# Hardware loops for VectorE and ScalarE in a decode attention kernel

## The chip, the cores and the metric

One core of one Trainium2 chip. The time is the device time of one execution in microseconds (us), measured in several executions; the kernel before takes 1277.7 us. The groups of experiments ran on different chips; each had the kernel before beside it on its own chip. A profile is one execution taken by the hardware profiler; its span is some 2 us shorter than the device time of the same run (1276.2 against 1278.06 us before). Where a text below says "fill", it is one transfer of 8 MB of the K or V cache into a slot of the ring.

## The reference

A gated mix of two branches for two single tokens. Branch A is attention over a cache: 16 query heads, 8 KV heads, 32768 cached positions, head size 256. Branch B is a small MLP with GELU.

```python
def _A_ref(x, k_cache, v_cache, wq, wo):          # x [2, 1, 448]
    q = (x @ wq).reshape(B, Sq, 16, 256).transpose(0, 2, 1, 3)
    k = jnp.repeat(k_cache, 2, axis=1)             # k_cache, v_cache [2, 8, 32768, 256] bf16
    v = jnp.repeat(v_cache, 2, axis=1)
    p = softmax(einsum("bhqd,bhkd->bhqk", q, k) * 256 ** -0.5)
    return einsum("bhqk,bhkd->bhqd", p, v).transpose(0, 2, 1, 3).reshape(B, Sq, 4096) @ wo
# ... b = MLP(x);  g = sigmoid((x * gate_w).sum(-1));  return g * a + (1 - g) * b
```

The K and V caches are 537 MB; everything else is 10.6 MB. So each byte of the cache is read once and used for very little arithmetic.

## The kernel before

The 16 pairs of batch and KV head are 16 "groups". A group has two K tiles and two V tiles of 8 MB. All of them pass through a ring of three slots in SBUF, loaded by SyncE in the order K2, V0, K3, V1 and so on. VectorE transposes the K tile in place (8 instructions), PE computes scores (`S`), VectorE and ScalarE do the softmax, PE multiplies with V (`PV`), VectorE picks out the result (`do_end`), and at the very end PE multiplies with wo (`FIN`).

Each engine's program is made by one Python function. Only PE's has a hardware loop in the kernel before: `loop` runs the body once in Python for the instructions, and waits use a register of the loop for the semaphore's value. The other engines' programs are unrolled.

```python
# _Eng.wait: inside a loop the value waited for is computed from the loop's register
if self.at is not None:
    nm, v0, d = next(self.at[1])
    self.eng.wait_ge(st.sem, self.at[0] * d + v0)
    return
# ... PE: 5 passes of 6 tiles, which is 3 groups
E.loop((NTILES - LAG) // UNIT, steps, ("dve", ("PT", 0)))
# ... VectorE, unrolled over all 64 tiles
for kind, idx in order:
    if kind == "K":
        for blk in range(NCK):
            T(idx, blk)                       # transpose in the ring
        if idx % NT == NT - 1:
            softmax(idx // NT)
    elif kind == "V" and idx % NT == NT - 1:
        do_end(idx // NT)
# ... ScalarE, unrolled over the 16 groups
for g in range(NG):
    chain(g)                                  # exp of the scores
    if g + 1 < NG:
        fill_A(g + 1)                         # 8 small copies of q for the next group's scores
# ... SyncE: a fill is issued when PE has released what lay in its slot
for d in order:
    for pd in before_of[d]:
        E.wait("pe", released(pd))            # K: last scores of the tile; V: last PV of the tile
```

## Time and profile before

| | before |
|---|---|
| time, median of 3 runs | 1277.68 us |
| span of the profiled run | 1276.2 us |
| read from HBM | 547.43 MB, 429 GB/s over the span |
| load queue (q1) | 99.4% of 16 engines' time |
| PE, VectorE, ScalarE busy | 57%, 54%, 3% |

The page of the profile gives the span, the busy time of each engine, then rows of 40 equal slices (tenths of busy time for the DMA engines, and GB/s), then for each DMA queue its packets, MB and share, then the engines of the chain that ended last.

```profile
span 1276.2 us, 8103 instructions
...
PE 725.7 (57%) x4683; PEld 165.2 (13%) x2155; DVE 690.8 (54%) x545; ACT 42.4 (3%) x182; POOL 2.5 (0%) x11
...
DMA  9999999999999999999999999999999999999997
GB/s 410 428 432 434 438 431 428 438 430 438 433 427 436 433 438 433 429 435 433 434 431 435 431 438 429 435 433 429 442 428 435 435 427 436 435 433 435 427 429 300
...
q1 hardware_dynamic: 12328, 547.43, 99.4%
q8 instruction: 9, 0.15, 0.0%
q14 instruction: 7, 0.06, 0.0%
...
DMA 58%; DVE 21%; PE 18%; ACT 2%; issue 1%; SPq 0%; another core or an unknown queue 0%
...
```

The load queue q1 is busy all the time and delivers 427 to 442 GB/s in each slice but the first and the last. Two queues called "instruction" also move bytes: the program itself, as the experiments will show (longer unrolled code raises q14's count from 7 to 14 or 15, PE's loop unrolled q8's from 9 to 27). They have 0.21 MB together, a share that rounds to 0.0%.

How far ahead are the loads? SyncE's timeline shows when fills were issued (start, duration of the issue, engine and line), VectorE's when a K tile's transposes began. Both are of the kernel before; in brackets stands how long the engine idled before an instruction and what ended that.

```profile
...
304.18 0.33 SPq L373 DMA_DIRECT2D ring<-in_A_k_cache_dram  x1
332.76 0.33 SPq L373 DMA_DIRECT2D ring<-in_A_v_cache_dram  x1
336.33 0.33 SPq L373 DMA_DIRECT2D ring<-in_A_k_cache_dram  x1
...
```

```profile
...
304.19 1.25 DVE L720 STREAM_TRANSPOSE PT<-pexp 128x1024 bf16<-128x1024 bf16 x1 [4.74 <-PE ps_o L322]
...
310.53 0.23 DVE L748 TENSOR_TENSOR attnT<-ps_m,rl 128x2 bf16<-128x2 f32 x2 [1.10 <-PE ps_m L492]
311.37 17.66 DVE L700 STREAM_TRANSPOSE ring<-ring 128x2048 uint32<-128x2048 uint32 x8 [0.60 <-DMA ring<-in_A_k_cache_dram]
350.06 11.08 DVE L700 STREAM_TRANSPOSE ring<-ring 128x2048 uint32<-128x2048 uint32 x5 [21.03 <-DMA ring<-in_A_k_cache_dram]
```

The K fill that is ahead of the V fill issued at 332.76 us lands at 350.06 us, when the transposes of its tile begin after 21 us of waiting for it. Only then is it the V fill's turn. So this fill was issued 17.3 us early, and a delay shorter than that should change nothing.

### The profile page before, as it was taken

The numbers are of one execution on the slowest core, as the hardware profiler recorded it, in microseconds if no ns is written. First come the engines' busy times: TensorE is split into PE (matmuls) and PEld (weight loads), VectorE is DVE, ScalarE is ACT, GpSimd is POOL, SyncE is SP. The second block draws the span as 40 slices with busy tenths as digits, with TensorE's granted clock in tenths as the row PEclk, the third lists the DMA queues.
The fourth block names the chain that finished last, engine by engine and source line by source line (L and its number), as shares of the span: only waits on it lengthen the run. The fifth ranks groups of instructions, "written<-read, shape, count | busy, mean of one in ns | idle before, by whom it ended". The sixth has DMA issues, their size and how long they took to land.

```text
span 1276.2 us, 8103 instructions
## 1 busy us (share of the span) xinstructions
PE 725.7 (57%) x4683; PEld 165.2 (13%) x2155; DVE 690.8 (54%) x545; ACT 42.4 (3%) x182; POOL 2.5 (0%) x11
## 2 busy tenths in 40 slices
PE   3566665645576454765536656455763547655464
PEld 3111111101011010111101111011110101111011
DVE  2775546745366553555735467453675535656351
ACT  1000000000000000000000000000000000000000
POOL 0000000000000000000000000000000000000000
PEclk9987887777887677887768877778886777876786
DMA  9999999999999999999999999999999999999997
GB/s 410 428 432 434 438 431 428 438 430 438 433 427 436 433 438 433 429 435 433 434 431 435 431 438 429 435 433 429 442 428 435 435 427 436 435 433 435 427 429 300
DMA packets 12520, 547.64 MB, mean 429 GB/s; under 512 B 1364, under 2 KB 3544, under 8 KB 3672
## 3 DMA queue, kind: packets, MB, share of 16 engines
q1 hardware_dynamic: 12328, 547.43, 99.4%
q8 instruction: 9, 0.15, 0.0%
q14 instruction: 7, 0.06, 0.0%
q10 hardware_dynamic: 176, 0.01, 0.0%
HBM read 547.43 MB, written 0.00 MB: 429 GB/s over the span
## 4 chain that ended last, share of the span: by engine, by line
DMA 58%; DVE 21%; PE 18%; ACT 2%; issue 1%; SPq 0%; another core or an unknown queue 0%
DMA ring<-in_A_k_cache_dram 56%; DVE ring L700 18%; PE ps_s L463 5%; PE ps_s L322 5%; PE ps_o L322 5%; DMA ring<-in_A_wo_dram 3%; PE ps_o L523 2%; DVE mx L704 1%; ACT pexp L616 1%; PE ps_m L485 1%; PE ps_m L480 1%; PE ps_m L475 0%; DVE gmax L706 0%; DVE ls L715 0%; DVE gmx L710 0%
## 5 line engine op out<-in xcount | busy, mean ns | idle before, releaser
L700 DVE STREAM_TRANSPOSE ring<-ring 128x2048 uint32<-128x2048 uint32 x256 | 565.1, 2275 | 319.2 <-DMA ring<-in_A_k_cache_dram 319.2
L463 PE MATMUL ps_s<-ring,Abd 128*128 128x512 bf16 x1024 | 428.9, 419 | 372.4 <-DVE ring L700 372.1
L322 PE MATMUL ps_s<-ring,Abd 128*128 128x512 bf16 x1024 | 425.3, 415 | 0.0
L463 PEld LDWEIGHTS ps_s<-ring,Abd 128*128 128x128 bf16 x1024 | 106.6, 104 | 786.2 <-DVE ring L700 410.9
L322 PE MATMUL ps_o<-ring,PT 128*24 128x512 bf16 x1504 | 128.4, 454 | 0.0
L523 PE MATMUL ps_o<-ring,PT 128*24 128x512 bf16 x544 | 64.8, 476 | 11.1 <-DMA ring<-in_A_v_cache_dram 11.1
L720 DVE STREAM_TRANSPOSE PT<-pexp 128x1024 bf16<-128x1024 bf16 x16 | 19.9, 1244 | 81.0 <-PE ps_o L322 81.0
L492 PE MATMUL ps_m<-sel,o_sb 128*128 128x2 f32 x64 | 16.2, 358 | 80.2 <-DVE o_sb L742 80.2
L742 DVE SCALAR_TENSOR_TENSOR o_sb<-ps_o,mask,o_sb 128x256 f32<-128x256 f32 x112 | 54.1, 483 | 9.6 <-PE ps_o L523 5.7
L704 DVE TENSOR_REDUCE mx<-ps_s 128x1 f32<-128x1024 f32 x16 | 19.6, 1224 | 60.1 <-PE ps_s L322 60.1
L612 ACT ACTIVATE negm<-ps_m 128x1 f32<-128x1 f32 x16 | 2.7, 171 | 1161.2 <-PE ps_m L480 1161.2
L523 PEld LDWEIGHTS ps_o<-ring,PT 128*24 128x24 bf16 x544 | 15.8, 107 | 119.7 <-issue 104.8
L492 PEld LDWEIGHTS ps_m<-sel,o_sb 128*128 128x128 f32 x64 | 14.9, 320 | 98.9 <-DVE o_sb L742 98.7
L485 PE MATMUL ps_m<-ls,ones_f 128*128 128x2 f32 x32 | 8.2, 325 | 28.2 <-DVE ls L715 28.2
L715 DVE TENSOR_SCALAR ls<-par,lsum 128x2 f32<-128x2 f32 x16 | 3.7, 228 | 31.1 <-ACT pexp L616 31.1
L475 PE MATMUL ps_m<-ident_f,mx 128*1 128x128 f32 x32 | 6.1, 270 | 23.6 <-DVE mx L704 23.6
L607 ACT COPY Abd<-qrep 32x16 bf16<-32x16 bf16 x128 | 19.4, 198 | 0.6
L616 ACT ACTIVATE pexp<-ps_s,negm 128x1024 bf16<-128x1024 f32 x16 | 17.8, 1114 | 0.5
L748 DVE TENSOR_TENSOR attnT<-ps_m,rl 128x2 bf16<-128x2 f32 x32 | 3.7, 158 | 21.2 <-PE ps_m L492 21.2
L739 DVE TENSOR_SCALAR o_sb<-ps_o,mask 128x256 f32<-128x256 f32 x16 | 7.1, 446 | 14.2 <-PE ps_o L322 14.2
L480 PE MATMUL ps_m<-ones_f,gmx 1*128 1x1 f32 x32 | 6.6, 271 | 9.9 <-DVE gmx L710 9.9
L485 PEld LDWEIGHTS ps_m<-ls,ones_f 128*128 128x128 f32 x32 | 6.8, 265 | 29.6 <-DVE ls L715 29.6
(65 smaller groups left out, 67.9 us busy)
## 6 DMA issues: line engine op xcount, KB each, us to landing
ring<-in_A_v_cache_dram SPq DMA_DIRECT2D x1, 4096.0 KB, 28.0
ring<-in_A_v_cache_dram SPq DMA_DIRECT2D x2, 2048.0 KB, 34.7
ring<-in_A_wq_dram SPq DMA_DIRECT2D x1, 3072.0 KB, 10.2
ring<-in_A_wo_dram SPq DMA_DIRECT2D x1, 1792.0 KB, 32.3
ring<-in_B_w_dram SPq DMA_DIRECT2D x1, 1568.0 KB, 18.0
ring<-in_B_w_dram SPq DMA_DIRECT2D x1, 1344.0 KB, 13.8
ring<-in_A_wo_dram SPq DMA_DIRECT2D x1, 1344.0 KB, 35.3
ring<-in_A_wq_dram SPq DMA_DIRECT2D x1, 512.0 KB, 11.0
```

The costliest lines, as they stand in the source:

```text
L322: return e.add_instruction(mybir.InstMatmult(name=f"I-{nc.next_id()}", engine=mybir.EngineType.PE, ldweights=False, ins=[e.lower_ap(x), e. ...
L463: fn = lambda e, o=o, x=x, st=st, sp=sp, s=s, w=w: e.matmul(o, a_win(s, w), x, start=st, stop=sp, skip_group_check=True)
L480: E.ins(lambda e: e.matmul(ps_m[:, C_BC:C_BC + 1], gmx[:, :], ones_f[0:1, 0:1], start=True, stop=True), key=("M2", g))
L485: E.ins(lambda e: e.matmul(ps_m[:, C_L:C_L + 2], ones_f[:, :], ls2[:, :], start=True, stop=True), key=("L", g))
L492: E.ins(lambda e, j=j: e.matmul(ps_m[:, C_OT + 2 * j:C_OT + 2 * j + 2], o_sb[:, j:Dh:2], sel[:, :], start=True, stop=True), key=(("OT", g) ...
L523: fn = lambda e, o=o, x=x, wt=wt, st=st, sp=sp, j=j: e.matmul(o, wt, x, start=st, stop=sp, skip_group_check=True)
L607: E.ins(lambda e, o=o, Q=Q, c=c: e.copy(o[:, :, c:c + 2], qrep[32 * Q:32 * Q + 32, :, kvh, :, b]), key=(("A", g) if (Q == 3 and c == 16) e ...
L616: E.ins(lambda e: e.activation(pexp[:, :].rearrange("p (r i a) -> p i r a", r=CR, i=2), ps_s[:, :].rearrange("p (i r a) -> p i r a", i=2, ...
L700: E.ins(lambda e: e.transpose(k_words(idx, blk), k_words(idx, blk)), key=("T", idx, blk))
L704: E.ins(lambda e: e.tensor_reduce(mx[:, :], ps_s[:, :], AX.X, ALU.max), key=("MX", g))
L720: E.ins(lambda e: e.transpose(PT[:, :], pexp[:, :]), key=("PT", g))
L742: E.ins(lambda e, p=p, m=m: e.scalar_tensor_tensor(out=o_sb[:, :], in0=p, scalar=m, in1=o_sb[:, :], op0=ALU.mult, op1=ALU.add), key=(("OS" ...
```

## The change

VectorE gets a hardware loop of 5 passes of three groups, as PE has; ScalarE one of 14 passes of one group. The columns of `qrep` (read by ScalarE) and `attnT` (written by VectorE) that belong to a group must then be an address computed from the loop's register. For that both tiles are laid out so that a step of one group is a constant step in columns. The two products that write `attnT` become one of four columns, for which sums and reciprocals are four wide and the latter's tile is threefold. The intent is a shorter program.

```diff
+    def dyn(self, base, step):
+        return base if self.at is None else self.at[0] * step + base
...
-        qrep = sb("qrep", [P, NS, Hkv, 2, Bn], dt.bfloat16)
+        qrep = sb("qrep", [P, NS, 2 * NG], dt.bfloat16)
-        attnT = sb("attnT", [P, Hkv, 2, 2, Bn], dt.bfloat16)
+        attnT = sb("attnT", [P, 4 * NG], dt.bfloat16)
...
 # PE, final product: the two weight columns are now 64 bytes apart
-   ps_a[32 * q:32 * q + Bn, :], attnT[:, kvh, j, hh, :],
+   ps_a[32 * q:32 * q + Bn, :], attnT[:, 4 * kvh + 2 * j + hh:4 * NG:4 * Hkv],
...
 # ScalarE
-   E.ins(lambda e, ...: e.copy(o[:, :, c:c + 2], qrep[32 * Q:32 * Q + 32, :, kvh, :, b]), ...)
+   E.ins(lambda e, ...: e.copy(o[:, :, c:c + 2],
+                               qrep[32 * Q:32 * Q + 32, :, bass.ds(E.dyn(2 * g, 2), 2)]), ...)
-            for g in range(NG):
-                chain(g)
-                if g + 1 < NG:
-                    fill_A(g + 1)
+            def step(n):
+                chain(n + 1)
+                fill_A(n + 2)
+            chain(0)
+            fill_A(1)
+            E.loop(NG - 2, step, ("dve", ("PT", 0)))
+            chain(NG - 1)
...
 # VectorE
-                for j in range(2):
-                    E.ins(lambda e, j=j: e.tensor_tensor(
-                        attnT[:, kvh, j, :, b], ps_m[:, C_OT + 2 * j:C_OT + 2 * j + 2], rl[g % 2][:, :], ALU.mult), ...)
+                E.ins(lambda e: e.tensor_tensor(attnT[:, bass.ds(E.dyn(4 * g, 4 * UNIT // NT), 4)],
+                                                ps_m[:, C_OT:C_OT + 4], rl[g % 3][:, :], ALU.mult), key=("O", g))
-            for kind, idx in order: ...
+            for i in range(LAG):
+                K(i)
+            E.loop((NTILES - LAG) // UNIT, steps, ("dve", ("PT", 0)))
+            do_end(NG - 1)
```

(Cut: the four-wide `par`, `ls2`, `rl` and `L`, and waits on constants inside a loop.)

More of the change, by code (lines that the diff above doesn't have):

```diff
@@ L59, in loop @@
             v0 = v[1] - d
-            assert v0 > 0 and d > 0 and all(v[i] == v0 + i * d for i in range(1, n)), reqs
+            assert v0 > 0 and d >= 0 and all(v[i] == v0 + i * d for i in range(1, n)), reqs
             assert v[0] in (None, v0) or (nm == first[0] and v0 < v[0] <= ev[first[1]]), reqs
@@ L93, in wait @@
             assert nm == stream
-            self.eng.wait_ge(st.sem, self.at[0] * d + v0)
+            self.eng.wait_ge(st.sem, self.at[0] * d + v0 if d else v0)
             return
@@ L226, in bass_gated_mix__gqa_block_cached__dense_activation_gelu__decode_kernel @@
         sel = sb("sel", [P, 2], dt.float32)
-        par = sb("par", [P, 2], dt.float32)
+        par = sb("par", [P, 4], dt.float32)
         mx = sb("mx", [P, 1], dt.float32)
@@ L232, in bass_gated_mix__gqa_block_cached__dense_activation_gelu__decode_kernel @@
         lsum = sb("lsum", [P, 1], dt.float32)
-        ls2 = sb("ls2", [P, 2], dt.float32)
-        rl = [sb(f"rl{i}", [P, 2], dt.float32) for i in range(2)]
+        ls2 = sb("ls2", [P, 4], dt.float32)
+        rl = [sb(f"rl{i}", [P, 4], dt.float32) for i in range(3)]
         ps_s = pm("ps_s", [P, 1024], dt.float32)
@@ L484, in L @@
                 E.wait("dve", ("LS", g))
-                E.ins(lambda e: e.matmul(ps_m[:, C_L:C_L + 2], ones_f[:, :], ls2[:, :],
+                E.ins(lambda e: e.matmul(ps_m[:, C_L:C_L + 4], ones_f[:, :], ls2[:, :],
                                          start=True, stop=True), key=("L", g))
@@ L593, in prog_act @@
             E.wait("pe", "QR")
-            E.ins(lambda e: e.copy(qrep[:, :, :, :, :].rearrange("p s v h b -> p s (v h b)"), ps_qr), key="qr")
+            E.ins(lambda e: e.copy(qrep[:, :, :].rearrange("p s (b n) -> p s n b", b=Bn),
+                                   ps_qr.rearrange("p s (n b) -> p s n b", b=Bn)), key="qr")
             E.wait("act", "qr")
@@ L606, in fill_A @@
                     for c in (0, 16):
-                        E.ins(lambda e, o=o, Q=Q, c=c: e.copy(o[:, :, c:c + 2], qrep[32 * Q:32 * Q + 32, :, kvh, :, b]),
+                        E.ins(lambda e, o=o, Q=Q, c=c: e.copy(o[:, :, c:c + 2],
+                                                            qrep[32 * Q:32 * Q + 32, :, bass.ds(E.dyn(2 * g, 2), 2)]),
                               key=(("A", g) if (Q == 3 and c == 16) else None))
@@ L639, in prog_dve @@
             E.ins(lambda e: e.tensor_reduce(sel[:, :], ident_f[:, :].rearrange("p (c h) -> p h c", h=2), AX.X, ALU.add), key="sel")
-            E.ins(lambda e: e.tensor_reduce(par[:, :], ident_f[:, :].rearrange("p (k h) -> p h k", h=2),
-                                            AX.X, ALU.add), key="par0")
-            E.wait("dve", "par0")
-            E.ins(lambda e: e.tensor_scalar(par[:, :], par[:, :], 0.5, None, op0=ALU.mult), key="par")
+            E.wait("dve", "sel")
+            for j in range(2):
+                E.ins(lambda e, j=j: e.tensor_scalar(par[:, 2 * j:2 * j + 2], sel[:, :], 0.5, None, op0=ALU.mult),
+                      key=("par" if j else "par0"))
             E.wait("pool", "xm0")
@@ L716, in softmax @@
                 E.wait("pe", ("L", g))
-                E.ins(lambda e: e.reciprocal(rl[g % 2][:, :], ps_m[:, C_L:C_L + 2]), key=("RL", g))
+                E.ins(lambda e: e.reciprocal(rl[g % 3][:, :], ps_m[:, C_L:C_L + 4]), key=("RL", g))
                 if g >= 1:
@@ L725, in do_end @@
                     E.wait("pe", ("PV", g * NT + NT - 1))
-                if g >= 1:
-                    E.wait("pe", ("OT", g - 1))
+                E.wait("pe", ("OT", g - 1))
                 for n in range(8):
@@ L746, in do_end @@
                 E.wait("dve", ("RL", g))
-                for j in range(2):
-                    E.ins(lambda e, j=j: e.tensor_tensor(
-                        attnT[:, kvh, j, :, b], ps_m[:, C_OT + 2 * j:C_OT + 2 * j + 2], rl[g % 2][:, :], ALU.mult),
-                        key=(("O", g) if j == 1 else ("O0", g)))
+                E.ins(lambda e: e.tensor_tensor(attnT[:, bass.ds(E.dyn(4 * g, 4 * UNIT // NT), 4)],
+                                                ps_m[:, C_OT:C_OT + 4], rl[g % 3][:, :], ALU.mult), key=("O", g))
             gelu1()
@@ L754, in prog_dve, with K, steps @@
             do_bp()
-            for kind, idx in order:
-                if kind == "K":
-                    for blk in range(NCK):
-                        T(idx, blk)
-                    if idx % NT == NT - 1:
-                        softmax(idx // NT)
-                elif kind == "V" and idx % NT == NT - 1:
-                    do_end(idx // NT)
+            def K(idx):
+                for blk in range(NCK):
+                    T(idx, blk)
+                if idx % NT == NT - 1:
+                    softmax(idx // NT)
+            def steps(n):
+                for i in range(UNIT * n, UNIT * n + UNIT):
+                    K(i + LAG)
+                    if i % NT == NT - 1:
+                        do_end(i // NT)
+            for i in range(LAG):
+                K(i)
+            E.loop((NTILES - LAG) // UNIT, steps, ("dve", ("PT", 0)))
+            do_end(NG - 1)
             E.wait("pe", "FIN")
```

## The prediction

> **What bounds it.** The transfers. The page's header and its DMA queue part show 547.4 MB read in 1276.2 us, the load queue busy for 99.4% of 16 engines' time; in the 40-slice view DMA is 9 in all slices but the last. Four fills of the ring (33.55 MB) take 77.4 us (transposes of K tiles start at 195.26 and 272.66 in the timeline): 433.5 GB/s. [...] VectorE is busy 54%, ScalarE 3%. The chain of waits gives DMA 58%.
>
> **The margin of the queue.** A V fill is issued at 332.76 us; the K fill ahead of it lands at 350.06: 17.3 us early. Others I followed: V fills 17 to 18 us, K fills some 26, the last V tile 18 (issued 1225.45, its turn at 1243.7), wo 27. VectorE idles about 34 us of each 77.4 us group. So a delay within a group is paid back by idle time unless it passes some 17 us, and does not add up.
>
> **What the change does.**
> - VectorE: 5 passes of 3 groups, ScalarE: 14 of one; waits and two addresses come from registers. The trace times no register work. PE already loops 5 times; at its turn (310.5 to 315.9 us) there is only a wait for VectorE, so a turn costs under 5.4 us there. My estimate for VectorE: under 5 us for a turn and under 4 us of register work along a group's chain (about 20 waits), together below 17.
> - Two 158 ns products per group become one: 0.1 us of VectorE per group. Sums and reciprocal are 4 wide instead of 2 (228 and 170 ns: same). Setup of `par` hides under the wq load.
> - ScalarE: 8 copies per group (1.25 us together) with a register column. Even at 0.3 us more each, Abd, ready at 144.9 us, is first read at 161: 16 us of margin.
> - Instruction fetch: 0.21 MB on instruction queues, 0.5 us at 433 GB/s. Shorter program or refetch: within 0.3 us either way.
> - Tail: the last load lands at 1271.44, then 1.73 us of matmuls, 0.33 mix, 2.6 store. The last product ends at 1271.02, off the path by 0.4 us; one instruction instead of two: 0.07 us earlier. The final matmuls read two weight columns 64 bytes apart instead of adjacent; 64 loads of 22 ns follow the last landing: 0 to 0.5 us.
>
> **On the critical path:** practically nothing; -0.3 to +0.7 us.
>
> **Prediction:** 1277.7 us, 8 in 10 between 1275 and 1281. Faster by over 2%: 0.01; within 2%: 0.97; slower by over 2%: 0.02.
>
> **What would show it.** Load queue still about 99.4%, 433 GB/s in every middle slice. Issue to landing of the fills (46.7 us K, 36.6 V median) shorter by the loop's delay, a few us, but well above 19.3 us, the time of one fill. VectorE busy about 2 us less; new small gaps before its transposes after each third group and before each small softmax operation. The last load lands within 1 us of 1271.4.
>
> **What would make it wrong.** A turn or register waits costing over 17 us (fetching the body behind the loads, say): then slices with DMA under 9 appear at the 5 turns, and the time grows by 5 times the excess. Strided weights costing much in the tail.

-0.3 to +0.7 us is 0 to 0.5 for the strided weights, 0.07 less for the product and 0.3 either way for the instruction fetch. The bounds for a turn, the register work and the strided weights were estimates.

## The result, and the profile after

| | before | after |
|---|---|---|
| time, median (range) of 4 runs | 1277.70 us (1277.58 to 1277.82) | 1275.64 us (1275.06 to 1276.38) |
| ratio, 95% interval | | 0.9984, 0.9967 to 1.0002 |
| span of the profiled run | 1276.2 us | 1274.3 us |
| VectorE busy | 690.8 us | 690.2 us |
| packets and MB on q14 | 7, 0.06 | 2, 0.02 |

A ratio is the mean time of one kernel's runs over that of the other's of the same rounds, so it is not quite the ratio of the medians. The interval just touches 1; a second group of five runs, below, gave 0.9984 again with 0.9970 to 0.9997. So there is a gain of 2 us, small and real, at the lower edge of what was predicted. The changed kernel's runs fall in two clusters, near 1275.1 and 1276.3.

The page of the kernel after, the same lines:

```profile
span 1274.3 us, 8475 instructions
...
PE 724.8 (57%) x4683; PEld 165.7 (13%) x2155; DVE 690.2 (54%) x529; ACT 43.3 (3%) x182; POOL 2.5 (0%) x11
...
DMA  9999999999999999999999999999999999999998
GB/s 411 428 432 433 438 433 430 434 435 431 434 432 430 440 434 430 436 430 430 442 432 432 434 430 430 442 432 432 434 432 430 440 432 432 434 432 430 440 423 323
...
q1 hardware_dynamic: 12328, 547.43, 99.5%
q8 instruction: 9, 0.15, 0.0%
...
q14 instruction: 2, 0.02, 0.0%
...
DMA 58%; DVE 18%; PE 18%; issue 4%; ACT 1%; ACTq 0%; SPq 0%; another core or an unknown queue 0%
...
```

The gain is not in VectorE's work. It comes in steps. The table of windows below (kernel before) is cut at the issue of the V fill that ends a group, so that each row is one group; it shows the window, its length, the busy time and count of instructions of PE, weight loads, VectorE, ScalarE and GpSimd, the granted clock, the DMA share and GB/s.

```profile
...
371.45:449.51 78.06, 43.96 (x266) 9.25 (x106) 42.67 (x32) 2.49 (x11) 0.00 (x0) 0.76 1.00 433
449.51:526.79 77.28, 44.12 (x266) 9.44 (x106) 42.57 (x32) 2.49 (x11) 0.00 (x0) 0.78 1.00 433
604.21:682.59 78.38, 43.56 (x266) 9.18 (x106) 42.66 (x32) 2.49 (x11) 0.00 (x0) 0.78 1.00 432
914.83:993.21 78.38, 43.56 (x266) 9.17 (x106) 42.67 (x32) 2.49 (x11) 0.00 (x0) 0.78 1.00 434
...
```

The same four groups of the kernel after:

```profile
...
371.46:448.86 77.40, 45.03 (x266) 9.46 (x106) 42.51 (x31) 2.49 (x11) 0.00 (x0) 0.76 1.00 434
448.86:526.27 77.41, 43.70 (x266) 9.33 (x106) 42.61 (x31) 2.49 (x11) 0.00 (x0) 0.78 1.00 433
603.67:681.08 77.41, 44.89 (x266) 9.47 (x106) 42.52 (x31) 2.48 (x11) 0.00 (x0) 0.76 1.00 433
913.27:990.67 77.40, 43.50 (x266) 9.30 (x106) 42.61 (x31) 2.48 (x11) 0.00 (x0) 0.78 1.00 434
...
```

After, every group takes 77.4 us. Before, three of these four groups are 0.7 to 1.0 us longer, while DMA share, PE and VectorE are as in the others. Something takes 1 us of the loads without showing up in their share.

The trace holds the landing times of each fill: its semaphore is raised 16 times, as many times as the page counts load engines. I sorted these 16 times for each fill, which the views of the profile don't do, and set them beside the start times of the instruction packets, which are in the trace too. "Lag" is the time from the first to the last of the 16.

```
fill   before: landed  step   lag   |  after: landed  step   lag
 19           369.39  19.35  1.86   |        369.40  19.36  2.10
 20           389.25  19.86  2.36   |        388.75  19.35  2.09
 32           621.50  19.36  2.39   |        620.95  19.35  2.04
 33           641.82  20.32  3.37   |        640.30  19.35  2.04
 48           932.12  19.36  3.41   |        930.56  19.36  1.98
 49           952.44  20.32  4.39   |        949.90  19.34  1.97
 63          1223.38  19.35  4.39   |       1220.82  19.35  1.91
 64          1243.69  20.31  5.35   |       1240.17  19.36  1.91
8 KB packets of q14 while the loads run, start in us:
before   86.89  301.90  385.39  625.87  934.07  1078.93  1239.83
after    91.24  302.65
```

All other fills from 20 to 64 take 19.33 to 19.37 us in both. The four steps of the kernel before (0.51, 0.97, 0.97 and 0.96 us) come in fills during which an 8 KB piece of the program was fetched (at 385.39, 625.87, 934.07 and 1239.83 us), and the lag grows by nearly the same amount each time: one load engine falls behind, the other fifteen do not. (The trace does not name the engine of a landing. But the second last of the 16 stays 1.8 to 1.9 us after the first in all eight fills of the kernel before, so it is one engine, and the same one, that is last.) (The pieces at 301.90 and 1078.93 us make no step. They are ScalarE's, as the experiments will show, and fell on an engine that was not the last: in the sorted times of the kernel before one landing falls back from 0.18 to 0.82 us after the first between fills 15 and 16, and from 0.78 to 1.38 us between fills 55 and 56.) In fill 64, the last whole one before the pieces of the tail, fifteen engines are within 1.9 us of each other, and one is 3.5 us behind these. By these numbers a packet of q14 holds up the loads of one engine, here by 0.5 to 1.0 us; how an engine shares its time between two queues was not shown. (PE's program comes on q8, as pe_flat below will show.)

A fill is 128 packets of 65536 bytes in the trace of the kernel before, and 15 of its 16 landings at fill 64 come within 1.9 us of each other; this fits an even split, 8 packets for each engine. So the last load ends when the slowest engine does. The end of the program then follows: in the kernel before the span ends 3.7 us after the last landing, in the kernel after and in after_again 3.8 us. The tail, seen on PE, before and then after:

```profile
...
1268.14 1.66 PE L537 MATMUL ps_f<-ring,attnT 128*2 128x112 bf16 x64 [3.01 <-DMA ring<-in_A_wo_dram]
1269.73 1.01 PE L492 MATMUL ps_m<-sel,o_sb 128*128 128x2 f32 x4
1271.44 1.73 PE L537 MATMUL ps_f<-ring,attnT 128*2 128x112 bf16 x64 [0.69 <-DMA ring<-in_A_wo_dram]
```

```profile
...
1264.64 1.66 PE L541 MATMUL ps_f<-ring,attnT 128*2 128x112 bf16 x64 [3.02 <-DMA ring<-in_A_wo_dram]
1266.23 1.01 PE L496 MATMUL ps_m<-sel,o_sb 128*128 128x2 f32 x4
1268.10 1.29 PE L541 MATMUL ps_f<-ring,attnT 128*2 128x112 bf16 x48 [0.85 <-DMA ring<-in_A_wo_dram]
1270.61 0.55 PE L541 MATMUL ps_f<-ring,attnT 128*2 128x112 bf16 x16 [1.22 <-DMA ring<-in_A_wo_dram]
```

64 final matmuls take 1.66 us in both (first line of each), so the weight columns that are now 64 bytes apart cost nothing. The last piece of wo landed at 1272.49 before and at 1270.48 after, by the landing times; fifteen of the engines were done at 1269.18 and 1269.17.

The loop itself shows in VectorE's timeline of the kernel after at the first turn, the jump back to the start of the body (the same place as shown of before):

```profile
...
305.02 1.25 DVE L730 STREAM_TRANSPOSE PT<-pexp 128x1024 bf16<-128x1024 bf16 x1 [5.32 <-PE ps_o L326]
...
311.57 0.16 DVE L756 TENSOR_TENSOR attnT<-ps_m,rl 128x4 f32 x1 [1.30 <-PE ps_m L496]
312.10 17.67 DVE L710 STREAM_TRANSPOSE ring<-ring 128x2048 uint32<-128x2048 uint32 x8 [0.36 <-issue]
350.07 11.08 DVE L710 STREAM_TRANSPOSE ring<-ring 128x2048 uint32<-128x2048 uint32 x5 [20.30 <-DMA ring<-in_A_k_cache_dram]
```

The turn leaves a gap of 0.36 us with the reason "issue"; the trace's compare-and-branch there takes 63 ns (56 to 67 at the four turns). The wait before the product, now with a computed address, went from 1.10 to 1.30 us. Along the whole chain of the group, which starts at the same time in both (294.06 and 294.04 us), the product starts 1.0 us later than before (311.57 against 310.53).

### The profile page after: what moved, and what is told of

The parts are those of the page before. It is cut to its first block, busy times and chain, and to the rows that moved or that the text cites. A ratio compares the mean times of both kernels' runs of the same rounds, so it can differ in the third digit from the quotient of the medians.

```text
span 1274.3 us, 8475 instructions
## 1 busy us (share of the span) xinstructions
PE 724.8 (57%) x4683; PEld 165.7 (13%) x2155; DVE 690.2 (54%) x529; ACT 43.3 (3%) x182; POOL 2.5 (0%) x11
## 3 DMA queue, kind: packets, MB, share of 16 engines
q1 hardware_dynamic: 12328, 547.43, 99.5%
HBM read 547.43 MB, written 0.00 MB: 430 GB/s over the span
## 4 chain that ended last, share of the span: by engine, by line
DMA 58%; DVE 18%; PE 18%; issue 4%; ACT 1%; ACTq 0%; SPq 0%; another core or an unknown queue 0%
DMA ring<-in_A_k_cache_dram 55%; DVE ring L710 16%; PE ps_s L467 5%; PE ps_s L326 5%; PE ps_o L326 5%; DMA ring<-in_A_wo_dram 3%; PE ps_o L527 2%; DVE mx L714 1%; PE ps_m L489 1%; PE ps_m L484 1%; PE ps_m L479 0%; ACT pexp L622 0%; DVE gmax L716 0%; DVE ls L725 0%; DVE gmx L720 0%
## 5 line engine op out<-in xcount | busy, mean ns | idle before, releaser
L496 PEld LDWEIGHTS ps_m<-sel,o_sb 128*128 128x128 f32 x64 | 14.9, 321 | 98.5 <-DVE o_sb L751 98.3
L489 PE MATMUL ps_m<-ls,ones_f 128*128 128x4 f32 x32 | 9.1, 354 | 29.4 <-DVE ls L725 29.4
L725 DVE TENSOR_SCALAR ls<-par,lsum 128x4 f32<-128x4 f32 x16 | 3.7, 229 | 32.6 <-ACT pexp L622 32.6
L612 ACT COPY Abd<-qrep 32x16 bf16 (+1 forms) x128 | 19.4, 198 | 0.6
L756 DVE TENSOR_TENSOR attnT<-ps_m,rl 128x4 f32 (+1 forms) x16 | 2.6, 162 | 24.2 <-PE ps_m L496 24.2
```

The source lines that it names most:

```text
L489: E.ins(lambda e: e.matmul(ps_m[:, C_L:C_L + 4], ones_f[:, :], ls2[:, :], start=True, stop=True), key=("L", g))
L496: E.ins(lambda e, j=j: e.matmul(ps_m[:, C_OT + 2 * j:C_OT + 2 * j + 2], o_sb[:, j:Dh:2], sel[:, :], start=True, stop=True), key=(("OT", g) ...
L612: E.ins(lambda e, o=o, Q=Q, c=c: e.copy(o[:, :, c:c + 2], qrep[32 * Q:32 * Q + 32, :, bass.ds(E.dyn(2 * g, 2), 2)]), key=(("A", g) if (Q = ...
```

## The experiments

Two theories stood against each other after the result, and two smaller ones. **Fetch**: what the loop saves is 8 KB pieces of VectorE's program, each of which costs about 1 us of one load engine, the same each time. **Layout**: the new layout saves time. **ScalarE**: its loop does. **Lottery**: chance of this load of the program. All kernels below gave correct results.

### Which part of the change gives the gain

Four kernels on one chip, 5 rounds each. `loop` is told to emit the passes one after the other for some engines; everything else stays as in the changed kernel.

```diff
     def loop(self, n, body, first):
         self.wait(*first)
+        if self.name in ('act', 'dve'):      # no_loop; ('act',) in dve_loop, ('dve',) in act_loop
+            for i in range(n):
+                body(i)
+            return
```

(Waits for events of a group before the first are skipped when unrolled.)

> The changed kernel again, as the control of this group. Fetch theory (each 8 KB piece of VectorE's program that is fetched while the loads run takes about 0.96 us of one load engine, always the same one, and the last load ends with its slowest engine): 1275.0 to 1276.4 us, ratio 0.998 to 0.999 to the kernel before; in the trace no instruction packet on queue 14 between 310 us and the end of the loads, and a spread of the 16 landings of a fill of about 2 us late in the run (5.3 us in the kernel before). Lottery rival (the 2 us is chance of this one load of the program): anywhere between 1275 and 1278.

> Changed layout, VectorE looped, ScalarE unrolled. Fetch theory: as the changed kernel, 1275.0 to 1276.5 us, since ScalarE's fetches (two, near 302 and 1079 us in the kernel before) hit another load engine that had 0.8 us and more to spare; VectorE's own fetches after 310 us are gone. Layout rival (the 2 us comes from the new layout of q and attention, not from loops): 1275.6. ScalarE rival (its loop is what helps): 1277.7.

> Changed layout, ScalarE looped, VectorE unrolled. Fetch theory: about as the kernel before, 1277.0 to 1278.0 us, with four or five fetches of 8 KB for VectorE and a spread of the landings of 4 to 5.4 us at the end of the loads. Layout rival and ScalarE rival: 1275.6.

> Changed layout, neither VectorE nor ScalarE looped. Fetch theory: as the kernel before, 1277.0 to 1278.0 us, spread of the landings 4 to 5.4 us at the end. Layout rival: 1275.6. If all four kernels of this group scatter over 1275 to 1278 without order, the lottery rival stands.

| | median (range), us | q14 packets from 310 us to the end of the loads | lag at fill 64 | span |
|---|---|---|---|---|
| before (9 runs beside) | 1277.54 (1277.33 to 1278.08) | 5 | 5.35 | 1276.2 |
| after_again | 1275.36 (1275.26 to 1276.28) | 0 | 2.38 | 1273.5 |
| dve_loop | 1274.98 (1274.89 to 1276.44) | 1 | 2.19 | 1273.2 |
| act_loop | 1277.82 (1277.68 to 1277.91) | 4 | 4.11 | 1276.0 |
| no_loop | 1277.62 (1277.47 to 1277.68) | 5 | 3.64 | 1275.7 |

(Packets, lag and span are of the profiled run; for before, of the profile above.) In act_loop and no_loop a last q14 packet at 1259 us brings the lag to 5.1 and 4.7 after fill 64. The layout alone gives nothing, ScalarE's loop gives nothing, VectorE's loop gives all of it: layout, ScalarE and lottery theories fall. dve_loop and after_again can't be told apart: each has runs in both clusters. The four also tell whose packets are whose: with ScalarE unrolled there are packets near 302 and 1077 us, with VectorE unrolled near 387, 688, 936 and 1259.

### Dose: more program, hardly more work

If the fetches are the cause, a longer program must cost time in proportion, although what it does costs the engine nothing that matters. Instructions that write one element were added; four kernels on one chip, 3 rounds.

```diff
 # bef_dve_pad (unrolled) and aft_dve_pad (in the loop): after the product of each group but the last
+                    for k in range(64):
+                        E.ins(lambda e, k=k: e.memset(junk[0:1, k:k + 1], 0.0))
 # bef_act_pad: at the end of fill_A
+                for k in range(64):
+                    E.ins(lambda e, k=k: e.copy(junk[0:1, k:k + 1], ident_f[0:1, 0:1]))
 # pe_flat: the changed kernel with PE's loop unrolled too
+        if self.name in ('pe',): ...
```

> The kernel before (VectorE unrolled) with 64 more one-element writes on VectorE after each group's last product, 15 times: 960 instructions, 60 KB more of program, which is 7.5 more fetches of 8 KB. Fetch theory: 7.5 times 0.96 us on the load engine that already ends last: 1277.6 + 7.2 = 1284.8 us (1283 to 1286), spread of the landings at the end of the loads about 12.5 us instead of 5.3. Rival that the time follows VectorE's own work and waits, or that instruction fetches are too few bytes to matter: unchanged, 1277.6 (the writes take about 4 us per group, inside the 17 us margin).

> The changed kernel (VectorE looped) with the same 64 writes per group, inside the loop. Fetch theory: if the body of some 300 instructions and their register work is kept on chip from pass to pass, 1275.3 to 1276.5; if it is fetched anew in each pass (about 3 pieces of 8 KB, 4 more passes), about 12 more fetches, up to 1287. Either way the time follows the count of queue 14's packets in the trace at 0.96 us each. Rival (VectorE's work): as for the other kernel with pads, the same change of time there and here.

> The kernel before with 64 more one-element copies on ScalarE after each fill of the block-diagonal tile, 16 times: 64 KB more of program, 8 more fetches of 8 KB. Fetch theory: ScalarE's fetches go to another load engine, that ended 4 us before the last one; 8 fetches at 0.6 to 1.0 us push it past by 1 to 4 us: 1278.5 to 1281.5 us, less than the same pads on VectorE cost. If all program fetches go to one engine: 1285. Rival: unchanged, 1277.6.

> The changed kernel with PE's loop unrolled: about 286 KB more of program, some 18 more fetches of 16 KB. In the trace so far each 16 KB fetch of PE delayed one load engine by about 1.5 us, each time another. Fetch theory with the engines taken in turn: 18 times 1.5 spread over 16 engines, about 1.7 us more for all: 1276.5 to 1279 us. If they all went to one engine: over 1295. If fetches don't matter: 1275.4.

| | median (range), us | ratio to before | q14 packets in the loads (before: 7) | q8 packets (before: 9) |
|---|---|---|---|---|
| bef_dve_pad | 1284.09 (1284.06 to 1284.56) | 1.0052 | 14 | 9 |
| aft_dve_pad | 1295.05 (1294.87 to 1295.22) | 1.0136 | 23 | 9 |
| bef_act_pad | 1279.46 (1279.39 to 1279.78) | 1.0015 | 15 | 9 |
| pe_flat | 1279.09 (1278.90 to 1279.61) | 1.0011 | 2 | 27 |

**bef_dve_pad.** 7 more packets, 6.4 us more. The 64 writes take 1.8 us of VectorE per group (timeline below). In the landing times, nine fills are 0.95 to 0.99 us longer than 19.35, each at one of the packets, and the lag at fill 64 is 11.74 us: one engine 9.5 us behind the other fifteen. The line of q14 on its page (packets, MB, share):

```profile
...
q14 instruction: 14, 0.11, 0.0%
...
```

**aft_dve_pad.** The same writes in the loop made it slower by 11 us than the same writes unrolled. The reason is in the same line: 23 packets against 14.

```profile
...
q14 instruction: 23, 0.19, 0.0%
...
```

The time follows the count: 20 packets between 310 us and the end of the loads against none in the changed kernel, 19.7 us more than its 1275.36, so 0.98 us each. (The changed kernel was not in this group; 1275.36 is from the chip where the kernel before took 1277.54 us, here it took 1277.70.) My guess of 12 packets was too low: the trace has five for each pass. VectorE's timeline of this kernel around a turn:

```profile
...
548.62 0.16 DVE L757 TENSOR_TENSOR attnT<-ps_m,rl 128x4 f32 x1 [1.30 <-PE ps_m L497]
548.72 1.79 DVE L761 MEMSET junk<- 1x1 f32 x64
558.27 2.31 DVE L711 STREAM_TRANSPOSE ring<-ring 128x2048 uint32<-128x2048 uint32 x1 [7.76 <-issue]
563.93 15.47 DVE L711 STREAM_TRANSPOSE ring<-ring 128x2048 uint32<-128x2048 uint32 x7 [3.35 <-issue]
```

At the turn VectorE itself now waits 7.8 us with the reason "issue", and 3.4 us more after the first transpose. So a body of 346 instructions (rows of one pass of VectorE in the trace) is fetched anew in each pass, some of it more than once by estimate (the 60 to 64 bytes per instruction worked out below make less than three packets, and five come). The wait alone is inside the margin of 17 us; the time is lost on the load engine. The lag at fill 64 is 7.6 us and not 20, because the other engines, up to 10.7 us ahead, ran out of issued loads soon after a turn (the first landings of fills 31, 43 and 55 come 4.5 to 4.8 us late, and the load queue's share fell to 98.3%). The last engine's fills are 0.9 to 1.0 or 2.9 us late, one packet or three.

**bef_act_pad.** 8 more packets, 1.8 us more. The line of q14:

```profile
...
q14 instruction: 15, 0.12, 0.0%
...
```

The steps of the landing times are 0.67 to 0.70 us here. Sorted, the landings of fill 64 show two laggards, one 6.9 us after the first engine (ScalarE's) and one at 4.0 (VectorE's); in the kernel before VectorE's was last and ScalarE's among the others. So the two programs are fetched by different load engines, and the cost shows only once its engine is the last.

**pe_flat.** 18 more pieces of 16 KB on q8, 3.7 us more than the changed kernel (again the 1275.36 us of the other chip). Its two instruction queues:

```profile
...
q8 instruction: 27, 0.44, 0.1%
...
q14 instruction: 2, 0.02, 0.0%
...
```

Eight engines end with a lag of 4.4 us or more in fill 64, eight with 2.1 us or less. The fills are late (by 1.5 to 1.7 us) only at fills 20, 41 and 63: after the 9th, 17th and 25th packet of q8. (The 1.5 us of the expectation: in the kernel before, with a packet of q8 at 62.61 us, one landing falls back from 0.39 to 1.94 us after the first between fills 3 and 4.) This fits PE's program being fetched by eight engines in turn, one about 1.6 us later each time (the trace does not name them); an estimate of 18 times 1.6 over 8 is 3.6 us, near the 3.7 measured. I had expected sixteen engines in turn and 1276.5 to 1279 us, and the median is just outside. 288 KB of program, spread over eight engines by this reading, cost PE less than 56 KB on one engine cost VectorE.

### How large may a loop's body be

The changed kernel's VectorE body has 154 rows in the trace and is not fetched again; 346 rows are. One more kernel has 26 writes per group in place of 64 (232 rows). And ScalarE's 64 copies went into its own loop (21 rows become 85).

```diff
 # aft_dve_pad26                                  # aft_act_pad: the changed kernel, at the end of fill_A
+                    for k in range(26):          +                for k in range(64):
+                        E.ins(... memset ...)    +                    E.ins(... copy ...)
```

> The changed kernel with 26 instead of 64 one-element writes on VectorE per group, inside the loop: a pass is 232 rows of VectorE in the trace, between the changed kernel's 154 (not fetched again) and 346 with 64 writes (about five fetches of 8 KB per pass, 1295 us). Fetch theory: the time follows the count of queue 14's packets, 1275.0 to 1276.5 us if a body of 232 stays on chip, and about 0.96 us more for each packet between 310 us and the end of the loads if not (12 to 20 packets: 1286 to 1295). It can't say which; this brackets the size of a free body. Rival that the writes themselves cost what the 64 cost: 26/64 of 19.7 us, 1283.4 us.

> The changed kernel with the 64 one-element copies on ScalarE inside its loop of one group per pass. The body is then some 80 instructions. Fetch theory, if such a body stays on chip from pass to pass as the changed kernel's VectorE body of some 145 instructions does: no fetches for ScalarE after 310 us, 1275.0 to 1276.5 us, against 1279.5 for the same copies unrolled. If it is fetched anew: as unrolled or slower, 1279 or more.

aft_dve_pad26: 1276.07 us (1275.04 to 1276.75), ratio 0.9990 (0.9973 to 1.0006); aft_act_pad: 1275.61 us (1274.70 to 1276.33), ratio 0.9982. Both stay with the changed kernel, and neither has a q14 packet between 310 us and the end of the loads. The line of q14 of aft_dve_pad26:

```profile
...
q14 instruction: 2, 0.02, 0.0%
...
```

78 writes more per pass cost nothing when the body is not fetched again (the rival's 1283.4 us is far off), and the same 64 copies of ScalarE that cost 1.8 us unrolled cost nothing in the loop. A body of 232 rows is free, one of 346 is not. In these runs VectorE's program comes in packets of 8192 bytes. Unrolled, it fetches one per four groups (625.87 to 934.07 us), and the windows count 32 instructions per group, so 64 bytes each (the 960 writes of bef_dve_pad took 7 packets more, 60 bytes each); by this estimate a body of 232 is 15 KB and is not fetched again, and one of 346 is 22 KB and is. Where between the two the limit lies, and what sets it, was not measured. (A row of the trace need not be exactly one instruction of the program.) PE, whose body of three groups is some 1100 rows (three times 266 and 106 in the windows), fetches at most one packet between its first turn and the tail in the kernels where it is looped.

### Is the margin of 17 us real

The prediction rests on it, so it was measured: VectorE gets two or five long reductions after each group's product, in the loop, which delays the next K tile's transposes. They add few instructions.

```diff
+                if g < NG - 1:
+                    for k in range(2):              # delay10; 5 in delay25
+                        E.ins(lambda e, k=k: e.tensor_reduce(
+                            junk[:, k:k + 1], PT[:, :].rearrange("p (n o) -> p n o", o=1).to_broadcast([P, 1024, 4]),
+                            AX.XY, ALU.max))
```

> The changed kernel with two more long reductions on VectorE after each group's product (4096 elements each; the row maximum takes 1.22 us for 1024, so an estimate of 4.9 us each): the next K tile's transposes start some 9.8 us later, 15 times. The prediction's margin theory: a V fill is issued some 17 us before its turn, so nothing changes: 1275.0 to 1276.5 us. Rival that VectorE's delays reach the end of the chain: up to 15 times 9.8 = 147 us more.

> The same with five reductions, some 24.5 us per group, still less than VectorE's idle time of 34 us in a group. Margin theory with 17 us: the V fill is issued 7 to 8 us after its turn, the load queue runs dry once per group, with about 2 us to get going again: 7 to 10 us for each of 14 or 15 groups, 1375 to 1425 us, and slices of the DMA row under 9. Rival that only VectorE's total time counts (68 of 77 us per group): unchanged, 1275.4.

delay10: 1275.20 us (1275.03 to 1276.48), ratio 0.9984: no change, with 131 us more of VectorE's time. delay25: 1330.31 us (1328.62 to 1331.09), ratio 1.0414. The line of the reductions in delay25 (busy us, mean ns), then DMA slices and load queue of its page, then SyncE's timeline:

```profile
...
L761 DVE TENSOR_REDUCE junk<-PT 128x1 f32<-128x4096 bf16 x75 | 325.7, 4409 | 0.0
...
```

```profile
...
DMA  9999989999899998999989999899998999989998
GB/s 402 435 441 433 427 348 410 443 414 437 342 423 443 411 443 348 443 433 421 439 344 419 443 411 443 356 435 439 415 443 348 421 433 411 443 371 419 429 425 333
...
q1 hardware_dynamic: 12328, 547.43, 96.3%
...
```

```profile
...
637.60 0.33 SPq L378 DMA_DIRECT2D ring<-in_A_k_cache_dram  x1
687.25 0.33 SPq L378 DMA_DIRECT2D ring<-in_A_v_cache_dram  x1
...
```

A reduction took 4.41 us, not 4.9, and five of them 21.7 us. The V fill at 687.25 us is issued 4.2 us after the queue ran dry (the K fill before it landed at 683.10 by the landing times), and it lands 6.6 us late (at 709.09): 21.8 us after its issue, where a fill that was queued in time takes 19.35, so 2.5 us went on getting going again. This is the margin of 17 us used up: 21.7 minus 16.6 (issue at 333.49 us and turn at 350.04 in the kernel after) is 5.1 us. The issue in the kernel after:

```profile
...
333.49 0.33 SPq L377 DMA_DIRECT2D ring<-in_A_v_cache_dram  x1
...
```

That there would be 7 to 10 us in each group was wrong: the loads themselves are then later by that much, and the trace has the long step in every second group only, with a step of about 1 us in between; so 55 us in place of 100 to 150.

## Why the prediction was right, and where not

- **Bound by the loads**: right. q1 has 99.4% before and 99.5% after, and 547.43 MB. A group reaches 433.5 GB/s (33.55 MB in 77.4 us), with the program on one core; what sets this rate was not shown.
- **Margin of 17 us, delays don't add up**: right, and measured by delay10 (8.8 us in each group: nothing) and delay25 (21.7 us: 55 us).
- **Loop turn under 5 us and register work under 4 us per group**: right and too careful: 0.36 us per turn, and 1.0 us along a group's chain, 0.2 of it before the product. The gaps that were to be seen are there. The fills' median from issue to landing, which was to be a few us shorter, is 45.8 us in place of 46.7 for K and the same 36.6 for V.
- **VectorE busy about 2 us less**: 0.6 us.
- **Tail**: strided weights cost nothing (64 final matmuls take 1.66 us in both). The time of the last landing was misread: matmuls start at 1271.44 when the last but one piece of wo lands; the last piece lands at 1272.49. After, it lands 2.0 us earlier, not within 1 us.
- **Instruction fetch, "0.5 us at 433 GB/s ... within 0.3 us either way"**: the term that was mis-sized. The mechanism was named, a shorter program saves fetches. But the bytes were divided by the rate of sixteen engines together. By the landings a fetch runs on one engine, VectorE's always on the same one, and 8 KB there take 0.96 us from the loads, not the 0.02 us of the sum. Four late fetches put this engine 3.5 us behind the others; the median gained 2.1 us, all of the change. The predicted -0.3 to +0.7 us was wrong; the range held because it was wider than the sum, which was luck as far as this term goes.

Of the 3.5 us, some is not seen at the end. In the profile of after the last engine is 1.3 us behind the other fifteen in the last piece of wo (1270.48 against 1269.17), in after_again 0.4 us (1269.66 against 1269.28). Both have one 16 KB packet of PE's program at 1268.3 to 1268.4 us. The spans of the changed kernel's runs, 1273.0 to 1273.5 or 1274.3 to 1274.4 us, differ by as much. That it is this packet, on an engine with or without work left, is argued and not shown. Open as well: why 8 KB cost 0.96 us on VectorE's engine and 0.67 on ScalarE's, when the engine moves 8 KB of loads in 0.30 us (524288 bytes per fill and engine in 19.35 us) and the packet itself is recorded with 0.33 us.

No version of these is clearly faster than the changed kernel. What could be left to gain on this line is an estimate of 2 us at most, the lag of the changed kernel.

## What to carry to other kernels

When loads are split evenly over all load engines and never pause, look at the slowest engine, not at the mean share: a transfer that is nothing in bytes can cost its full time if it always falls on the same engine. Program text was such a transfer here (0.96 us per 8 KB of VectorE's, of which VectorE itself saw nothing: no wait of it in the kernel before has the reason "issue"), so in a kernel bound by loads a hardware loop can pay on an engine that is half idle, if its body is not fetched again in each pass (232 rows were not, 346 were, and then the loop was worse than the unrolled code, 1295.05 against 1284.09 us). Here it paid 2 us of 1278 on VectorE, whose fetches fell on the last load engine, and nothing on ScalarE. Before costing delays, find how early the transfers are issued: here 17 us were free in each group, and past that delays reached the total (21.7 us per group cost 55 us in all).
